# Two of the first four token blocks turned by DMA, the first weights on ScalarE's queue, in a four-layer network of linear attention and gated MLPs

## Chip, cores, metric

The kernel runs on one core of a Trainium2 chip. The metric is the device time of one execution in microseconds (us), where lower is better. The profiler's span is about 1.8 us shorter than that time.

## The reference

The input is one sequence of 2048 tokens of 1024 bf16 values. Four layers follow each other, with a residual addition around each:

```python
x = x + A(layernorm(x), wqkv, wo)              # linear attention, 32 heads of 32
x = x + B(layernorm(x), W_gate, W_up, W_down)  # relu(x Wg) * (x Wu), then W_down; F = 3584
x = x + A(layernorm(x), wqkv, wo)
x = x + B(layernorm(x), W_gate, W_up, W_down)

def A(x, wqkv, wo):
    q, k, v = split_heads(x @ wqkv)
    pq, pk = phi(q), phi(k)                    # phi(t) = (t + 1 if t > 0 else exp(t)) + 1e-6
    kv = einsum("bhsd,bhse->bhde", pk, v); z = pk.sum(s)
    o = einsum("bhqd,bhde->bhqe", pq, kv) / (einsum("bhqd,bhd->bhq", pq, z) + 1e-6)
    return merge_heads(o) @ wo
```

## The kernel before

TensorE does the matmuls, VectorE and ScalarE the elementwise work, and SyncE and ScalarE issue the DMA transfers here. PSUM is the memory that TensorE's results are written to. Tokens are held in 16 blocks of 128, four blocks to a quarter. A block is normalized (two statistics instructions, a combination, two ScalarE steps for the reciprocal root, a scaling) and turned, so that features lie on partitions. Then a "unit" of eight matmuls projects one block onto 512 columns. k00 is block 0 on the first half of the key columns, k10 is block 1 on the same, q00 is block 0 on the first half of the query columns. The weight tiles are k0, k1, q0, q1 and v0, 1 MB each. x0 to x15 are the blocks' inputs, 256 KB each.

The change touches the head only. That is the first quarter of the first layer, some 40 us of 1629:

```python
# head(): idle matmuls, then the first loads
for _ in range(10):
    nc.tensor.matmul(idle, lhsT=zero[:, 0:P], rhs=zero, start=True, stop=True)
k0, k1, v0, q0, q1 = (ring.place() for _ in range(5))
self.load_x(0, 0, nc.scalar)          # half of x0, ScalarE's queue
self.load_x(0, 1)                     # other half, SyncE's queue
self.load_x(1, None, nc.scalar)
k0(0, H)                              # SyncE
self.load_x(2, None, nc.scalar)
k0(H, 2 * H)
self.load_x(3, None, nc.scalar)
k1(); q0()
self.load_x(4); ... ; self.load_x(7)
q1()
for t in range(8, self.ST): self.load_x(t)
v0()
...
# head_units(): the order of the work on blocks 0 to 3
def block0():
    stat(0, 0); stat(0, 1); rstd(0)
    stat(1, 0)                        # x1's first statistics AHEAD of x0's scaling
    scale(0, 0); scale(0, 1)
    t0 = turn(0, 0); t1 = turn(0, 1)  # transposes on TensorE, then copied out of PSUM
    ...
    k(0, 0, between)
def block(j, c, n):                   # used for n = 2 and 3
    scale(n)
    t0 = turn(n, 0); t1 = turn(n, 1)
    t0("s"); t1("s")
    if n + 1 < QT: norm(n + 1)
    k(j, c)
return [block0, block1, lambda: k(0, 1), lambda: block(1, 1, 2), lambda: k(2, 0),
        lambda: block(2, 1, 3), lambda: k(3, 0), lambda: k(3, 1)]
...
# quarter0(): the head units, then all eight query units of the first quarter
run(first)
run(column_major(q_unit, 0))
```

Blocks 4 to 15 are turned by DMA in both kernels (a DMA transpose issued by SyncE).

Of the kernel before, what the change touches and what calls it, by code (L numbers as in the profile page):

```python
# [15 lines left out]
QT = 4  # L16


class _Ring:
# [9 lines left out]
    def place(self):  # L29

        name, src = self.plan[self.loaded]
        t = self.pool.tile([P, 8, NW], BF16, tag="w")
        self.tiles[name] = t
        self.loaded += 1
        return lambda lo=0, hi=8: self.nc.sync.dma_start(out=t[:, lo:hi, :], in_=src[:, lo:hi, :])

    def load_to(self, n):
        while self.loaded < min(n, len(self.plan)):
# [40 lines left out]
class _Net:  # L79
# [131 lines left out]
    def head(self):  # L211

        nc, tc, ring = self.nc, self.tc, self.ring
        H = self.KT // 2

        zero = self.ep.tile([P, NW], BF16, tag="e")
        nc.vector.memset(zero, 0.0)
        idle = self.ps3.tile([P, NW], F32, tag="b")
        for _ in range(10):
            nc.tensor.matmul(idle, lhsT=zero[:, 0:P], rhs=zero, start=True, stop=True)  # L220

        k0, k1, v0, q0, q1 = (ring.place() for _ in range(5))
        self.load_x(0, 0, nc.scalar)
        self.load_x(0, 1)
        self.load_x(1, None, nc.scalar)
        k0(0, H)
        self.load_x(2, None, nc.scalar)
        k0(H, 2 * H)
        self.load_x(3, None, nc.scalar)
        k1()  # L230
        q0()
        self.load_x(4)
        self.load_x(5)
        self.load_x(6)
        self.load_x(7)
        q1()
        for t in range(8, self.ST):
            self.load_x(t)
        v0()
        src = self.xb  # L240
        self.xnT[0, 0] = self.xnTp.tile([P, self.KT, QT * P], BF16, tag="xnT", name="xnT0_0")
        stats = [self.small.tile([P, 2, nc.vector.BN_STATS_DIM], F32, tag="stats", name=f"st{j}")
                 for j in range(QT)]
        rs, xn = {}, {}

        def stat(j, c):
            self.ln_stat(j, src[j], c, stats[j])

        def rstd(j):
            rs[j] = self.ln_rstd(stats[j])  # L250
            xn[j] = self.xn_home(0, j)

        def scale(j, h=None):
            self.ln_scale(src[j], *rs[j], xn[j], h)

        def turn(j, h):
            tp = self.ps3.tile([P, H, P], BF16, tag="b")
            for i in range(H):
                kt = h * H + i
                nc.tensor.transpose(tp[:, i, :], xn[j][:, kt * P:(kt + 1) * P], self.ident)  # L260
            dst = self.xnT[0, 0][:, h * H:(h + 1) * H, j * P:(j + 1) * P]

            def take(engine):
                if engine == "v":
                    nc.vector.tensor_copy(out=dst, in_=tp)
                else:
                    nc.scalar.activation(out=dst, in_=tp, func=ACT.Copy)

            return take

        return stat, rstd, scale, turn

    def head_units(self, k, stat, rstd, scale, turn):

        def block0():
            stat(0, 0)
            stat(0, 1)
            rstd(0)
            stat(1, 0)
            scale(0, 0)  # L280
            scale(0, 1)
            t0 = turn(0, 0)
            t1 = turn(0, 1)
            t0("s")
            stat(1, 1)
            rstd(1)
            t1("v")
            k(0, 0, between)

        def between():  # L290

            scale(1, 0)
            t0 = turn(1, 0)
            scale(1, 1)
            t0("v")

        def block1():
            turn(1, 1)("v")
            norm(2)
            k(1, 0)  # L300

        def norm(j):
            stat(j, 0)
            stat(j, 1)
            rstd(j)

        def block(j, c, n):
            scale(n)
            t0 = turn(n, 0)
            t1 = turn(n, 1)  # L310
            t0("s")
            t1("s")
            if n + 1 < QT:
                norm(n + 1)
            k(j, c)

        return [block0, block1, lambda: k(0, 1), lambda: block(1, 1, 2), lambda: k(2, 0),
                lambda: block(2, 1, 3), lambda: k(3, 0), lambda: k(3, 1)]

    def ln_turn(self, layer, t, xn):  # L320
        nc = self.nc
# [60 lines left out]
    def layer_A(self, l, last_ln):  # L382
        nc, G, KT, D = self.nc, self.G, self.KT, self.D
        ring, later = self.ring, self.later
        H = D // NW
# [23 lines left out]
        def k_unit(q, j, c, between=None):  # L409
            t = q * QT + j  # L410
            pk = self.pk_home(l, t)
            self.phi(project(f"k{c}", q, j, between), pk[:, c * NW:(c + 1) * NW], "v")
            later.at(1 + (10 if self.phi_lag else 0), lambda: k_sum(t, slice(c * NW, (c + 1) * NW)))
# [54 lines left out]
        def q_unit(sc, j, c, lag=None):  # L468
            if c == 0 and (sc, j) not in pq_of:
                if sc < self.NQ - 1:  # L470
                    a = self.xnTp.tile([P, QT, D], BF16, tag="xnT", name=f"pq{l}_{sc}")
                    for i in range(QT):
                        pq_of[sc, i] = a[:, i, :]
                else:
                    pq_of[sc, j] = self.xnp.tile([P, D], BF16, tag="xn", name=f"pq{l}_{sc}_{j}")
            pq = pq_of[sc, j]
            self.phi(project(f"q{c}", sc, j), pq[:, c * NW:(c + 1) * NW], "s" if sc < self.NQ - 1 else "v")
            if c == H - 1 and lag is not None:
                later.at(lag, lambda: z_mult(sc, j))
# [61 lines left out]
        def column_major(f, q):  # L541
            return [lambda j=j, c=c: f(q, j, c) for c in range(H) for j in range(QT)]
# [4 lines left out]
        def run(*lists):  # L547

            n = max(len(u) for u in lists)
            for i in range(n):  # L550
                for u in lists:
                    if i < len(u):
                        u[i]()
                        later.tick()

        if l == 0:
            steps = self.head()
# [2 lines left out]
        for i in range(QT, self.ST):  # L560
            self.ln_at((8 if l == 0 else 2) + 3 * (i - QT), l, i, 2)
        if l == 0:
            first = self.head_units(lambda *a: k_unit(0, *a), *steps)
        else:
            first = column_major(k_unit, 0)

        def quarter0():
            self.phi_lag = 3 if l == 0 else 0
            run(first)
            run(column_major(q_unit, 0))  # L570
            later.at(1, lambda: None)
            self.phi_lag = 0

        if l == 0:
            with self.tc.manual_schedule(engines={mybir.EngineType.DVE,
                                                  mybir.EngineType.Activation}):
                quarter0()
        else:
            run(first, column_major(q_unit, 0))
# [160 lines left out]
```

## Time and profile before

| | kernel before |
|---|---|
| median of the runs ahead of the prediction | 1629.3 us (1629.21 to 1630.51) |
| the profiled run | 1630.68 us, span 1628.9 us |
| TensorE busy | 1621.7 us |
| TensorE idle, whole run | 7.2 us, of which 4.0 us in the first 10.3 us and 2.95 us after the last matmul |

The prediction shows the lines of the profile. To read them: a row of the timeline has the start, the duration, the engine, the source line, the operation and its tiles, the count, and in square brackets how long the engine had been idle and what ended that. A row of waits has who waited for whom, the total, the number of times and the longest, in us.

### The profile page before, as it was taken

What the parts mean: (1) busy time and instruction counts of PE and PEld (TensorE: products, weight loads), DVE (VectorE), ACT (ScalarE), POOL (GpSimd) and SP (SyncE); (2) the same over time, 40 slices, a digit from 0 to 9 for tenths busy, and PEclk for the clock granted to TensorE, in tenths of its full rate; (3) what the DMA queues carried; (4) which work ended last, traced back from release to release, by engine and by line L of the source; (5) the groups of instructions that cost most, each with busy time, mean ns of one, the idle gap of its engine ahead of it and who ended that gap; (6) DMA issues with size and microseconds to landing.
All of it is one profiled execution on the core that took longest, in us unless ns stands there. A gap on an engine that the chain in (4) does not pass through costs nothing.

```text
span 1628.9 us, 18772 instructions
## 1 busy us (share of the span) xinstructions
PE 1621.7 (100%) x7754; PEld 739.3 (45%) x7754; DVE 566.7 (35%) x940; ACT 331.8 (20%) x638; POOL 201.9 (12%) x134
## 2 busy tenths in 40 slices
PE   8999999999999999999999999999999999999999
PEld 4444444444444444444444444444444444444444
DVE  7845695213212222212165547942022111111211
ACT  5741212101110110111066312121011101101110
POOL 2349220000000000000023592100000000000000
DMA  7312647448445444544560147464554454454452
GB/s 245 65 52 56 178 71 206 144 148 232 155 143 190 160 151 161 168 147 137 168 128 1 53 93 250 85 193 146 182 165 152 155 184 155 145 166 154 155 162 71
DMA packets 298246, 235.06 MB, mean 144 GB/s; under 512 B 101296, under 2 KB 294192, under 8 KB 298160
## 3 DMA queue, kind: packets, MB, share of 16 engines
q1 hardware_dynamic: 292832, 228.75, 47.7%
q10 hardware_dynamic: 5328, 5.11, 0.9%
q8 instruction: 60, 0.98, 0.3%
q14 instruction: 26, 0.21, 0.0%
HBM read 201.33 MB, written 8.39 MB: 129 GB/s over the span
## 4 chain that ended last, share of the span: by engine, by line
PE 98%; ACT 1%; DVE 1%; DMA 1%; issue 0%; SPq 0%; DVEq 0%
PE pu L639 24%; PE pg L639 24%; PE acc L663 23%; PE ps L404 12%; PE ps L530 7%; PE ps L439 7%; DMA t<-in_A_wqkv_dram 1%; PE kv L452 0%; PE acc_last L663 0%; ACT e L351 0%; ACT e L350 0%; PE fold L515 0%; DVE st L138 0%; ACT e L352 0%; DVE slab L358 0%
## 5 line engine op out<-in xcount | busy, mean ns | idle before, releaser
L639 PEld LDWEIGHTS <-t 128*128 128x128 bf16 x3584 | 350.3, 98 | 423.2
L639 PE MATMUL pu<-xnT,t 128*128 128x512 bf16 x1792 | 423.5, 379 | 0.0
L639 PE MATMUL pg<-xnT,t 128*128 128x512 bf16 x1792 | 423.4, 379 | 0.0
L663 PE MATMUL acc<-t,hT 128*128 128x512 bf16 x1764 | 382.5, 379 | 0.0
L645 DVE TENSOR_TENSOR hT<-pu,rg 128x512 bf16<-128x512 f32 x224 | 154.7, 691 | 572.0 <-PE pu L639 572.0
L644 ACT ACTIVATE rg<-pg 128x512 f32<-128x512 f32 x224 | 133.5, 596 | 737.3 <-PE pg L639 737.0
L663 PEld LDWEIGHTS <-hT 128*128 128x128 bf16 x1820 | 177.9, 98 | 209.1
L404 PE MATMUL ps<-t,xnT 128*128 128x512 bf16 x1024 | 224.3, 380 | 2.2 <-DMA t<-in_A_wqkv_dram 1.7
L404 PEld LDWEIGHTS <-xnT 128*128 128x128 bf16 x1024 | 99.2, 98 | 122.3 <-issue 4.3
L530 PE MATMUL ps<-T,pqT 128*128 128x512 bf16 x512 | 111.2, 379 | 0.0
L145 ACT ACTIVATE rstd<-mv,eps 128x1 f32<-128x1 f32 x64 | 18.7, 293 | 334.1 <-DVE mv L143 333.9
L680 DVE TENSOR_TENSOR xo<-x,acc 128x512 bf16<-128x512 f32 x31 | 21.3, 688 | 170.3 <-PE acc L663 170.3
L483 POOL TENSOR_TENSOR prod<-pq,zrow 128x1024 f32<-128x1024 bf16 x32 | 67.9, 2122 | 85.9 <-DVE den L488 72.5
L138 DVE BATCH_NORM_STATS2 stats<-x 128x6 f32<-128x512 f32 (+1 forms) x120 | 78.0, 673 | 0.8
L530 PEld LDWEIGHTS <-pqT 128*128 128x128 bf16 x512 | 49.9, 98 | 60.4 <-issue 0.5
L419 POOL CAST ksum<-x 128x512 f32<-128x512 bf16 x2 | 1.7, 866 | 605.4 <-DVE x L358 605.4
L677 DVE TENSOR_TENSOR x<-x,acc 128x512 f32<-128x512 f32 x32 | 21.6, 675 | 138.5 <-PE acc L663 137.4
L421 POOL TENSOR_TENSOR ksum<-ksum,slab 128x512 f32<-128x512 f32 x46 | 54.0, 1183 | 84.6 <-DVE slab L358 75.1
L358 DVE SCALAR_TENSOR_TENSOR pq<-ps,e 128x512 bf16<-128x512 f32 x64 | 44.0, 688 | 53.9 <-ACT e L352 52.2
L495 POOL TENSOR_TENSOR pq<-pq,den 128x1024 bf16<-128x1024 bf16 x32 | 61.7, 1933 | 3.1 <-DVE den L490 3.1
L488 DVE TENSOR_REDUCE den<-prod 128x32 f32<-128x1024 f32 x32 | 39.0, 1217 | 53.9 <-POOL prod L483 53.9
L439 PE MATMUL ps<-slab,x 128*128 128x512 bf16 x256 | 56.6, 379 | 0.0
(57 smaller groups left out, 596.0 us busy)
## 6 DMA issues: line engine op xcount, KB each, us to landing
t<-in_B_W_gate_dram SPq DMA_DIRECT2D x56, 1024.0 KB, 7.1
t<-in_B_W_up_dram SPq DMA_DIRECT2D x56, 1024.0 KB, 5.4
t<-in_B_W_down_dram SPq DMA_DIRECT2D x64, 896.0 KB, 5.2
t<-in_A_wqkv_dram SPq DMA_DIRECT2D x11, 1024.0 KB, 5.6
t<-in_A_wo_dram SPq DMA_DIRECT2D x4, 1024.0 KB, 7.2
away<-x SPq DMA_DIRECT2D x8, 512.0 KB, 4.4
x<-away SPq DMA_DIRECT2D x8, 512.0 KB, 8.5
out_dram<-xo ACTq DMA_DIRECT2D x31, 128.0 KB, 2.5
```

Of the source, the lines that this page charges most:

```text
L138: self.nc.vector.bn_stats(out=stats[:, c, :], in_=src[:, c * fmax:(c + 1) * fmax])
L358: nc.vector.scalar_tensor_tensor(out=out, in0=ps, scalar=0.0, in1=e, op0=ALU.max, op1=ALU.add)
L404: nc.tensor.matmul(by_row(ps), lhsT=self.xnT[l, l_q][:, kt, j * P:(j + 1) * P], rhs=w[:, kt, :].rearrange("p (b i d) -> p i b d", i=R, d=H ...
L421: nc.gpsimd.tensor_tensor(out=ksum[:, cols], in0=ksum[:, cols], in1=pk, op=ALU.add)
L439: nc.tensor.matmul(ps, lhsT=self.xn[l, t][:, d * P:(d + 1) * P], rhs=self.pk[l, t][:, h * NW:(h + 1) * NW], start=(t == 0), stop=(t == sel ...
L483: nc.gpsimd.tensor_tensor(out=prod, in0=pq_of[sc, j], in1=zrow, op=ALU.mult)
L495: nc.gpsimd.tensor_tensor(out=heads(pq), in0=heads(pq), in1=den[:, :].unsqueeze(2).to_broadcast([P, D // HD, HD]), op=ALU.mult)
L530: nc.tensor.matmul(ps, lhsT=pqT[sc][:, g, j * P:(j + 1) * P], rhs=T[g // 2][:, g % 2, n2 * NW:(n2 + 1) * NW], start=(g == 0), stop=(g == G ...
L639: nc.tensor.matmul(ps, lhsT=w[:, kt, fi * P:(fi + 1) * P], rhs=self.xnT[l, q][:, kt, :], start=(kt == 0), stop=(kt == KT - 1))
L644: nc.scalar.activation(out=rg, in_=pg, func=ACT.Relu)
L645: nc.vector.tensor_tensor(out=h[:, fi, :], in0=pu, in1=rg, op=ALU.mult)
L663: nc.tensor.matmul(ps[:, 0:n], lhsT=hT[ft // 4][:, ft % 4, j * P:(j + 1) * P], rhs=wd[:, k, i * n:(i + 1) * n], start=(ft == 0), stop=(ft ...
```

## The change

The intent is to give the first weights the DMA engines early, to take 16 transposes off TensorE, and to have other work (two query units) ready while blocks 2 and 3 are turned by DMA. Cut to the core:

```diff
         k0, k1, v0, q0, q1 = (ring.place() for _ in range(5))
-        self.load_x(0, 0, nc.scalar)
+        self.load_x(0, 0)
         self.load_x(0, 1)
-        self.load_x(1, None, nc.scalar)
-        k0(0, H)
-        ... (x2, x3 on ScalarE's queue; k0, k1, q0, x4 to x15, q1, v0 on SyncE's)
+        self.load_x(1)
+        nc.vector.memset(ring.get((0, "k0"))[:, 0, 0:2], 0.0)
+        k0(0, H, nc.scalar)
+        k0(H, 2 * H, nc.scalar)
+        k1(0, 2 * H, nc.scalar)
+        q0(0, 2 * H, nc.scalar)
+        def load(n):
+            if n == 0:
+                nc.vector.memset(self.xb[2][:, 0:2], 0.0)   # holds x2 back
+                self.load_x(2)
+                self.load_x(3)
+                return
+            for t in range(4, 8):
+                self.load_x(t)
+            q1()
+            for t in range(8, self.ST):
+                self.load_x(t)
+            v0()
...
         def block0():
             stat(0, 0)
+            load(0)
             stat(0, 1)
...
-        def block(j, c, n):            # ... transposes on TensorE
+        def turned(n):
             scale(n)
+            self.ln_turn(0, n, xn[n])  # DMA transpose
-        return [block0, block1, lambda: k(0, 1), lambda: block(1, 1, 2), ...]
+        return ([block0, block1, lambda: (turned(2), norm(3), k(0, 1)),
+                 lambda: (turned(3), load(1), k(1, 1)), lambda: q(0, 0), lambda: q(1, 0)]
+                + [lambda f=f, j=j, c=c: f(j, c) for j in (2, 3) for f, c in ((k, 0), (k, 1), (q, 0))]
+                + [lambda j=j: q(j, 1) for j in range(QT)])
```

SyncE's order in this stretch is now the program's own, as VectorE's and ScalarE's were already.

More of the change, by code (lines that the diff above doesn't have):

```diff
@@ L34, in place @@
         self.loaded += 1
-        return lambda lo=0, hi=8: self.nc.sync.dma_start(out=t[:, lo:hi, :], in_=src[:, lo:hi, :])
+        return lambda lo=0, hi=8, queue=None: (queue or self.nc.sync).dma_start(
+            out=t[:, lo:hi, :], in_=src[:, lo:hi, :])
     def load_to(self, n):
@@ L222, in head @@
         k0, k1, v0, q0, q1 = (ring.place() for _ in range(5))
-        self.load_x(0, 0, nc.scalar)
+        self.load_x(0, 0)
         self.load_x(0, 1)
-        self.load_x(1, None, nc.scalar)
-        k0(0, H)
-        self.load_x(2, None, nc.scalar)
-        k0(H, 2 * H)
-        self.load_x(3, None, nc.scalar)
-        k1()
-        q0()
-        self.load_x(4)
-        self.load_x(5)
-        self.load_x(6)
-        self.load_x(7)
-        q1()
-        for t in range(8, self.ST):
-            self.load_x(t)
-        v0()
+        self.load_x(1)
[16 more added lines that the diff above has]
+            v0()
         src = self.xb
@@ L269, in turn, with head_units @@
             return take
-        return stat, rstd, scale, turn
-    def head_units(self, k, stat, rstd, scale, turn):
+        return load, xn, stat, rstd, scale, turn
+    def head_units(self, k, q, load, xn, stat, rstd, scale, turn):
         def block0():
             stat(0, 0)
+            load(0)
             stat(0, 1)
@@ L305, in norm @@
             rstd(j)
-        def block(j, c, n):
+        def turned(n):
             scale(n)
-            t0 = turn(n, 0)
-            t1 = turn(n, 1)
-            t0("s")
-            t1("s")
-            if n + 1 < QT:
-                norm(n + 1)
-            k(j, c)
-        return [block0, block1, lambda: k(0, 1), lambda: block(1, 1, 2), lambda: k(2, 0),
-                lambda: block(2, 1, 3), lambda: k(3, 0), lambda: k(3, 1)]
+            self.ln_turn(0, n, xn[n])
[3 more added lines that the diff above has]
+                + [lambda j=j: q(j, 1) for j in range(QT)])
     def ln_turn(self, layer, t, xn):
@@ L562, in layer_A @@
         if l == 0:
-            first = self.head_units(lambda *a: k_unit(0, *a), *steps)
+            first = self.head_units(lambda *a: k_unit(0, *a), lambda *a: q_unit(0, *a), *steps)
         else:
@@ L569, in quarter0 @@
             run(first)
-            run(column_major(q_unit, 0))
-            later.at(1, lambda: None)
             self.phi_lag = 0
         if l == 0:
-            with self.tc.manual_schedule(engines={mybir.EngineType.DVE,
+            with self.tc.manual_schedule(engines={mybir.EngineType.DVE, mybir.EngineType.SP,
                                                   mybir.EngineType.Activation}):
```

## The prediction

> **What bounds the kernel now.** I read the page first (busy shares and chain), then the wait totals, then the timeline of the first 22 us, because the change touches nothing later, and last the landings of the single loads in that stretch.
>
> ```profile
> PE 1621.7 (100%) x7754; PEld 739.3 (45%) x7754; DVE 566.7 (35%) x940; ACT 331.8 (20%) x638; POOL 201.9 (12%) x134
> ...
> PE 98%; ACT 1%; DVE 1%; DMA 1%; issue 0%; SPq 0%; DVEq 0%
> ```
>
> TensorE is busy for 1621.7 of 1628.9 us. All the idle time there is to win is 7.2 us, 0.44%. The whole-run waits say where TensorE spends it:
>
> ```profile
> PE ps L404 <- DMA t<-in_A_wqkv_dram: 1.7, 1, 1.7
> PE idle L220 <- DVE zero L217: 1.3, 1, 1.3
> ...
> PE tp L260 <- DVE x L154: 0.6, 1, 0.6
> ...
> PE ps L404 <- ACT xnT L267: 0.4, 1, 0.4
> ```
>
> These sum to 4.0 us. The chain of waits ends its matmuls at 1625.95, so 2.95 us more are the tail, the last addition and store, which the change does not touch. Of 7.2 us only the 1.7 us wait for the first weights and the 0.6 and 0.4 us ahead of the first block are within the change's reach. The timeline shows that stretch:
>
> ```profile
> 6.38 0.72 PE L260 MATMUL tp<-ident,x 128*128 128x128 bf16 x8 [0.58 <-DVE x L154]
> ...
> 7.46 1.04 PE L404 MATMUL ps<-t,xnT 128*128 128x512 bf16 x4 [0.37 <-ACT xnT L267]
> ...
> 10.23 0.59 PE L404 MATMUL ps<-t,xnT 128*128 128x512 bf16 x2 [1.73 <-DMA t<-in_A_wqkv_dram]
> ...
> 11.56 3.74 PE L404 MATMUL ps<-t,xnT 128*128 128x512 bf16 x16
> ...
> 15.13 0.61 PE L260 MATMUL tp<-ident,x 128*128 128x128 bf16 x8
> ...
> 15.58 3.62 PE L404 MATMUL ps<-t,xnT 128*128 128x512 bf16 x16
> ...
> 19.28 0.62 PE L260 MATMUL tp<-ident,x 128*128 128x128 bf16 x8
> ```
>
> Four matmuls of the first unit use the first half of weight tile k0, then 1.73 us are lost until the second half lands. The two groups of 8 transposes at 15.13 and 19.28 are those of blocks 2 and 3. The next projection starts at 15.58 and at 19.74, so each group holds TensorE for 0.45 us. A projection unit of 8 matmuls takes 1.73 us (0.216 us each).
>
> The landings of the two halves of k0 (queries on the load line, cut to one or two loads each) are:
>
> ```profile
> L35 SPq DMA_DIRECT2D t<-in_A_wqkv_dram x1: 419/419/419, 1.2 to 1.2; - x1
> DMA to landing us min/median/max: 4.5/4.5/4.5
> ...
> L35 SPq DMA_DIRECT2D t<-in_A_wqkv_dram x2: 419/460/500, 1.2 to 1.7; - x2
> DMA to landing us min/median/max: 4.5/6.5/8.5
> ```
>
> So k0's halves landed at 5.7 and 1.66 + 8.5 = 10.2 us. The same query gives, for the others: k1 2.2 + 11.2 = 13.4, q0 3.6 + 12.8 = 16.4; blocks of tokens x1 5.2, x2 1.7 + 7.7 = 9.4, x3 2.2 + 8.2 = 10.4, x4 5.75 + 11.3 = 17.05. The windows of 1 us show the DMA at 302 to 388 GB/s from 3 us on: it is saturated, and which bytes go first decides who waits. Note the third unit, the first to use k1: it follows the second unit at about 13.4, just as k1 lands. So k1 is nearly a bound already.
>
> **What the Trainium skill says.** "DMA: Bandwidth & Descriptors", section "Issuing engines are not separate DMA queues": transfers started by ScalarE and SyncE run on the same 16 engines and interleave; a second issuer saves issue time only. The trace agrees: two queues were in use and the sum stayed below 390 GB/s. The same page, "Queues, rings and completion order": an engine alternates between queues packet by packet, and completion is not first-in-first-out. The trace agrees: k0's second half was complete only when 2.8 MB had moved (sum of the windows to 10.2 us), although just 2.1 MB (four blocks and k0) had been asked for ahead of it or with it. The same page, "Rules for kernel authors": a transpose next to ordinary DMAs needs nothing, only two transposing queues must be kept apart. Here all are issued from SyncE; the first transpose of the trace landed after 4.1 us with loads in flight, a later one after 3.0. "TensorE: Matmul & The Clock Gate", Part 4, puts a transpose at about 275 ns in one kernel; here 8 hold TensorE for 0.45 us together, so 56 ns each, and the measurement decides.
>
> **The change part by part.**
> 1. Blocks 2 and 3 are turned by DMA. TensorE loses 16 transposes: 2 x 0.45 = 0.90 us, all on its path. ScalarE loses 4 copies (two pairs of 1.08 us), off the path.
> 2. The order becomes k00, k10, k01, k11, q00, q10 (six units on blocks 0 and 1), then k, k, q of block 2, of block 3, then the four second-half query units. The same 16 units; in the instruction order of the changed kernel TensorE differs only by the 16 transposes. ScalarE's three-step query work (0.60 + 0.63 + 0.72 = 1.95 us a unit, above 1.73) is now mixed with one-step key units; before, it ran 8 in a row and the only gap later in the head, 0.11 us at 44, may be its effect. Gain 0.1.
> 3. Weights k0, k1, q0 go on ScalarE's queue; x0 and x1 go on SyncE's, x2 and x3 are held back by a tiny memset until the first statistics (about 4.3 us: x0's half lands at 3.54, plus 0.65 of statistics and the memset). The first half of k0 waits for a memset too, so it starts at about 1.4 instead of 1.19.
>
> Landings by my estimate: fit to the before landings, the slowest engine moves as if the whole ran at 0.30 MB/us from 2.1 us, plus 0.6 us to land (k0b: 2.1 MB gives 9.7, seen 10.2; k1: 3.15 MB gives 13.2, seen 13.4; q0: 4.2 MB gives 16.7, seen 16.4). After, k0b needs 1.57 MB (x0, x1, k0) plus 0 to 0.5 of x2 and x3: 7.9 to 9.7. k1 needs 2.6 to 3.15 MB: 11.4 to 13.2. q0 needs 4.2 MB and has no x4 beside it: about 16.4.
>
> Now TensorE's clock. k00 starts at about 7.5 (x1 is issued 0.35 us later and its statistics stand ahead of x0's scaling, so 0 to 0.3 later, partly balanced by earlier statistics of x0). Without a wait for k0b, k00 and k10 with block 1's transposes (2 x 0.22) end at 7.46 + 3.46 + 0.44 = 11.4. k01 needs k1: at 12.8, a new wait of about 1.4. k01 and k11 end at 16.3; q00 needs q0 at 16.4. q00 and q10 end at 19.9. Block 2's first unit starts there. Before, six units with the same transposes plus those of two blocks were done at 19.74 + 1.73 = 21.47. Gain 1.5 us, plus the 0.1: 1.6. Had the weights been there in time it would have been 1.73 + 0.90 + 0.1 = 2.7.
>
> Is block 2 turned by 19.9? x2 issued at 4.3 lands perhaps at 10 (the 4.0 to 7.7 us of x1 and x2 before). Then statistics 1.28, combining 0.21, the two ScalarE steps 0.5, scaling 0.55: scaled at 12.6; DMA transpose 4.1 to 4.7 us under load: 17.3. Slack 2.6 us. Block 3 is scaled near 16, turned near 20, needed at 25. But VectorE's order puts the statistics of blocks 2 and 3 ahead of freeing the first unit's PSUM: x2's landing + 5.2, so 15.2, needed by q00 at 16.4. If x2 lands at 12, this costs 0.7. The loads of x4 on are held until block 3's transpose is issued (about 17 instead of 5.75): x4 lands near 20.5, its statistics come at about 21.7; q1 lands near 26, needed at 30.3. Both fit, with 1 and 4 us of slack.
>
> I take off 0.1 for such small losses: gain 1.5 us. 1629.3 - 1.5 = 1627.8.
>
> **The rivals.**
> - The wait only moves: k0b's 1.7 us is given back in full at k1 and q0, because the same 4.2 MB are needed and now the query weights are asked for about 5 us sooner (after four units, not eight). For it: q0's 16.4. It leaves the transposes' share or less: gain 0.5 to 1, about 1628.6.
> - VectorE or the DMA transposes become the bound: x2 held back by 2.6 us lands at 12 to 13 (7.7 after issue), PSUM comes free late or block 2 is late. Against it: x2 stands first in an empty SyncE queue. Gain 0 to 0.5, or a loss up to 1: 1629 to 1630.
> - The transfers go better than the estimate: 4.2 MB at the mean 365 GB/s would have q0 by 14.2, k1 by about 11.5. Gain 2.7, 1626.6.
> - The late start of x4 to x15 stalls the second quarter. Against it: 12 blocks, q1 and v0 (5.2 MB) take about 15 us from 19, so land by 35, and the second quarter starts at 37.
>
> **Range and chances.** The bound of 2.7 us gives 1626.6 at best, a full loss gives 1629.3, and a bad head 1630; the three runs before spread by 1.3 us. Range 1626.3 to 1629.6. Two per cent is 32.6 us: the change can't win that, as only 7.2 us are idle, and I see nothing in it to lose as much, so within 2% at 0.985.
>
> **What would show it.** Right: TensorE busy falls by 0.9 us; the 1.7 us wait for weights shrinks to under 0.6 in the first unit and one of about 1 us appears at the third; the sixth unit ends near 20. Wrong: a TensorE wait on the transposed tile at the seventh unit (block 2 late), on VectorE's join at the fifth (PSUM), a first unit starting after 8, or the third unit starting at 11.5 without a wait (then the gain is near 2.7).

## The result

| | before | changed |
|---|---|---|
| median of 4 runs | 1629.32 us (1629.21 to 1630.51) | 1632.71 us (1630.74 to 1634.47) |
| granted clock, run by run | | 0.999, 0.998, 1.000, 0.999 |
| ratio changed / before | | 1.0019, interval 1.0001 to 1.0036 |

The change did not gain 1.5 us. It lost about 3, and the predicted range, which ended at 1629.6, does not hold the median. The spread grew with it, to 3.7 us.

The busy share of TensorE in the changed kernel, from the page:

```profile
PE 1621.6 (99%) x7738; PEld 739.7 (45%) x7738; DVE 566.9 (35%) x942; ACT 331.1 (20%) x634; POOL 201.9 (12%) x134
```

There are 16 matmuls fewer, but busy time fell by only 0.1 us, where the prediction had 0.9 less. Other matmuls must have run more slowly. The waits of TensorE in the first 60 us of the changed kernel:

```profile
PE tp L267 <- DVE x L155: 2.1, 1, 2.1
...
PE ps L408 <- DMA xnT<-x: 1.9, 1, 1.9
...
PE idle L221 <- DVE t L228: 1.3, 1, 1.3
...
PE ps L408 <- ACT xnT L274: 0.4, 1, 0.4
...
PE ps L408 <- DVE slab L362: 0.3, 1, 0.3
```

The 1.7 us wait for weights is gone, and no wait for weights took its place. Instead the wait ahead of the first transposes grew from 0.6 to 2.1 us. A wait of 1.9 us for a tile turned by DMA is new, and so is 0.3 us for VectorE (PSUM not yet freed). TensorE's timeline of the changed kernel puts them in place:

```profile
1.35 4.04 PE L221 MATMUL idle<-zero 128*128 128x512 bf16 x10 [1.35 <-DVE t L228]
7.51 0.72 PE L267 MATMUL tp<-ident,x 128*128 128x128 bf16 x8 [2.13 <-DVE x L155]
8.60 2.74 PE L408 MATMUL ps<-t,xnT 128*128 128x512 bf16 x6 [0.37 <-ACT xnT L274]
...
12.28 5.35 PE L408 MATMUL ps<-t,xnT 128*128 128x512 bf16 x24
17.98 21.15 PE L408 MATMUL ps<-t,xnT 128*128 128x512 bf16 x96 [0.35 <-DVE slab L362]
41.03 69.24 PE L408 MATMUL ps<-t,xnT 128*128 128x512 bf16 x320 [1.90 <-DMA xnT<-x]
110.11 8.80 PE L443 MATMUL ps<-slab,x 128*128 128x512 bf16 x40
```

The same stretch in the kernel before, from its sixth unit on:

```profile
19.74 88.70 PE L404 MATMUL ps<-t,xnT 128*128 128x512 bf16 x408
108.27 8.80 PE L439 MATMUL ps<-slab,x 128*128 128x512 bf16 x40
```

The last row of each is the stage after the keys and queries. Before, it started at 108.27, now at 110.11, which is 1.84 us later. The spans differ by 1.9 us (1628.9, 1630.8). So all of the difference arises ahead of this stage, and its start can serve as the measure in the experiments.

Three things are to be seen. First, the start: the first transposes begin at 7.51 instead of 6.38. VectorE's timeline says why:

```profile
4.41 0.21 DVE L144 BATCH_NORM_AGGREGATE mv<-st 128x2 f32<-128x12 f32 x1
...
6.45 0.69 DVE L139 BATCH_NORM_STATS2 st<-x 128x6 f32<-128x512 bf16 x1 [1.83 <-DMA x<-in_A_x_dram]
7.06 0.72 DVE L155 TENSOR_SCALAR x<-x,mv,rstd 128x512 bf16<-128x512 bf16 x2
```

x0 was ready to be scaled at about 5.2. VectorE waited until 6.45 for x1, whose statistics stand ahead in its order. x1 was third on SyncE's queue, issued at 1.66 and landed 4.8 us later. Before, it was second on ScalarE's queue and landed at 5.2.

Second, six projection matmuls take 2.74 us, where the same six before took 1.04 + 0.59 besides the wait. The 1 us windows of the changed kernel show the granted TensorE clock as the column behind the five engines:

```profile
8.00:9.00 1.00, 0.63 (x5) 0.19 (x4) 0.88 (x3) 0.85 (x3) 0.00 (x0) 0.63 1.07 371
9.00:10.00 1.00, 1.00 (x4) 0.44 (x3) 0.73 (x2) 0.19 (x1) 0.00 (x0) 0.50 1.04 363
10.00:11.00 1.00, 1.00 (x4) 0.30 (x3) 0.00 (x0) 0.00 (x0) 0.00 (x0) 0.50 1.09 358
11.00:12.00 1.00, 1.00 (x7) 0.67 (x6) 0.20 (x1) 0.00 (x0) 0.00 (x0) 0.67 1.09 347
```

Together (0.37 + 0.50 + 0.50 + 0.33) / 0.5 = 3.4 us at half clock. Third, the 17th unit, the first of block 4, waits for its turned block. The first DMA transpose of block 4 in the kernel before, then in the changed one, by duration of the issue (ns), time of issue, and time to landing:

```profile
L326 SPq DMA_TRANSPOSE xnT<-x x1: 1347/1347/1347, 27.2 to 27.2; - x1
DMA to landing us min/median/max: 4.1/4.1/4.1
```

```profile
L330 SPq DMA_TRANSPOSE xnT<-x x1: 4813/4813/4813, 31.7 to 31.7; - x1
DMA to landing us min/median/max: 9.3/9.3/9.3
```

It was issued 4.5 us later and took 5.2 us longer, behind x8 to x15 and v0 in the same queue (v0 was issued at 30.95 and landed at 39.4). The late issue was not VectorE's doing, since block 4 was scaled by 27.9. SyncE works in order, and its own waits (20 to 46 us) show what held it:

```profile
SPq L373 <- DMA t<-in_A_wqkv_dram: 3.2, 1, 3.2
...
SPq L35 <- DMA x<-in_A_x_dram: 0.3, 1, 0.3
SPq L330 <- DMA x<-in_A_x_dram: 0.3, 1, 0.3
```

The program takes the semaphores of SyncE's DMAs from eight in turn, so each waits for the landing of the one eight places ahead of it. x15 waited for q1 (landed at 30.25), v0 for x8 (30.93), and the transpose for x9 (31.61). In the kernel before, the last of these waits ended at 23.5, before block 4 was ready (27.2).

From start to start, the two traces differ as follows, with 1.727 us a unit (8 x 0.2158):

| term | worked out | us |
|---|---|---|
| first transposes later | 7.51 - 6.38 | +1.13 |
| from there to k10, without the wait for weights | (12.28 - 7.51) - (11.56 - 6.38 - 1.73): half clock | +1.32 |
| no wait for k0's second half | | -1.73 |
| no 16 transposes | 2 x 0.45 | -0.90 |
| small waits around them, before | (19.74 - 11.56) - 4 x 1.727 - 0.90 | -0.37 |
| PSUM, changed | (17.98 - 12.28) - 3 x 1.727 | +0.52 |
| 17th unit late | 41.03 - (17.98 + 12 x 1.727) | +2.33 |
| later gaps, before less changed | 69.08 - (108.27 - 19.74 - 11 x 1.727) | -0.45 |
| sum | | +1.85 |

The measured sum is +1.84. The 17th unit's 2.33 is from start to start; the trace, which models the ends of matmuls, shows 1.90 of it as idle.

### The profile page after: what moved, and what is told of

It reads as the page before. It is cut to its first block, busy times and chain, and to the rows that moved or that the text cites. A ratio compares the mean times of both kernels' runs of the same rounds, so it can differ in the third digit from the quotient of the medians.

```text
span 1630.8 us, 18741 instructions
## 1 busy us (share of the span) xinstructions
PE 1621.6 (99%) x7738; PEld 739.7 (45%) x7738; DVE 566.9 (35%) x942; ACT 331.1 (20%) x634; POOL 201.9 (12%) x134
## 4 chain that ended last, share of the span: by engine, by line
PE 98%; DMA 1%; DVE 1%; ACT 0%; issue 0%; SPq 0%; DVEq 0%
PE pu L641 24%; PE pg L641 24%; PE acc L665 23%; PE ps L408 12%; PE ps L534 7%; PE ps L443 7%; DMA xnT<-x 1%; PE kv L456 0%; PE acc_last L665 0%; DMA x<-in_A_x_dram 0%; PE fold L519 0%; DVE x L155 0%; DVE st L139 0%; DVE slab L362 0%; DVE e L360 0%
```

## The experiments

The changed kernel was not timed in the call of e1 to e4, so their medians are set against it across calls, between which its own median moved from 1632.71 to 1634.22; their profiles are the firmer evidence. "Clock" counts the runs whose recorded mean granted clock was 1.000.

| run | edit, in words | median (low to high) | clock 1.000 | before on the same chip |
|---|---|---|---|---|
| e1_x1_early | changed, x1 ahead of the weights | 1630.32 (1629.36 to 1632.03) | 3 of 5 | 1630.00 (1629.42 to 1630.64) |
| e2_warm | changed, 19 idle matmuls | 1630.50 (1630.29 to 1631.40) | 5 of 5 | same |
| e3_loads_late | changed, last loads later | 1631.19 (1630.70 to 1632.68) | 1 of 5 | same |
| e4_both | e1 and e3 | 1630.51 (1629.09 to 1631.25) | 3 of 5 | same |
| after_again | changed, unaltered | 1634.22 (1632.30 to 1635.67) | 2 of 5 | 1629.37 (1629.27 to 1630.93) |
| e5_scale_first | changed, x0 scaled before x1's statistics | 1632.25 (1629.76 to 1632.81) | 2 of 5 | same |
| e6_before_hold | before, x2 and x3 held | 1630.56 (1628.88 to 1630.84) | 2 of 5 | same |
| e8_best | changed, repaired | 1629.16 (1629.06 to 1629.20) | 5 of 5 | same |
| before_a, before_b | before, unaltered, one look each | 1629.44; 1630.60 | 1.000; 0.999 | 1629.51 (1629.20 to 1630.70) |
| e9_best_nofill | e8 without its extra idle matmuls | 1629.19 (1628.65 to 1629.99) | 4 of 5 | same |
| e10_hold_warm | before, x2 and x3 held, 13 idle matmuls | 1629.32 (1628.93 to 1629.37) | 5 of 5 | same |
| after_c, d, e, f | changed, unaltered, one look each | 1631.36; 1630.43; 1629.17; 1632.22 | 0.999; 0.999; 1.000; 1.000 | 1630.08 (one run) |

### e1_x1_early: x1 ahead of the weights

```diff
         self.load_x(0, 0)
-        self.load_x(0, 1)
-        self.load_x(1)
+        self.load_x(0, 1, nc.scalar)
+        self.load_x(1, None, nc.scalar)
```

> The changed kernel with one edit: the second half of x0 and x1 are issued on ScalarE's queue ahead of the weights, as before the change. Theory (x1 late): in the changed kernel x1 landed at 6.45 instead of 5.2, VectorE's statistics of x1 stand ahead of the scaling of x0, so TensorE sat idle 2.13 us and then ran some 3.4 us at half clock. Then here x1 lands by 5.3, the first transposes start at 6.3 to 6.7 (7.51 in the changed kernel), the clock of the head is full, and the time falls by 1.1 to 2.5 us to about 1630.0; the wait of about 1.9 us for block 4's DMA transpose at the 17th unit stays, because VectorE's chain moves with the start. Rival (late start is bandwidth of the weights, whatever the queue): x1 still lands after 6 and the start stays above 7.3, time unchanged near 1632.5. Rival (the loss is all at the 17th unit): the start moves but the 17th unit starts at 41 as before, time unchanged.

In the profile x1 landed at 4.1, the first transposes began at 6.64, the clock was full, the stage after the keys began at 106.88 and the span was 1627.5 us. In that execution k01 waited 1.13 us for k1, as the prediction had it. The 1.9 us at the 17th unit did not stay, contrary to what was expected: block 4's transpose landed at 37.7. The other runs were less kind. Two of five, at clock 0.999, took 1631.7 and 1632.0. So the late x1 is a cause, but putting x1 first is no cure by itself. The timeline of this run shows a new cost:

```profile
1.68 3.89 ACTq L35 DMA_DIRECT2D t<-in_A_wqkv_dram  x4
...
4.63 0.21 DVE L144 BATCH_NORM_AGGREGATE mv<-st 128x2 f32<-128x12 f32 x1
...
5.61 0.29 ACT L146 ACTIVATE rstd<-mv,eps 128x1 f32<-128x1 f32 x1 [3.60 <-DVE st L139]
```

The statistics were ready at 4.84, but ScalarE was issuing q0, its last of six loads, until 1.68 + 3.89 = 5.57. An engine that issues loads does nothing else while it does.

### e2_warm: more idle matmuls

```diff
-        for _ in range(10):
+        for _ in range(19):
```

> The changed kernel with 19 idle matmuls at the start instead of 10, so that TensorE is busy until about 7.3 and the gap ahead of the first transposes shrinks from 2.1 us to under 0.5; nothing is issued or landed earlier. Theory (the idle gap makes the granted clock fall): the clock of the windows from 8 to 12 us is 1.00 instead of 0.5 to 0.67, the six first projection matmuls take 1.3 instead of 2.74 us, the granted clock of every run is 1.000, the time is 1630.7 to 1631.2 and the spread of the runs falls from 3.7 us to under 1. Rival (half clock comes by chance of the executions, not from this gap): clock and spread stay as they were, 1630.7 to 1634.5.

TensorE's timeline:

```profile
1.34 6.04 PE L221 MATMUL idle<-zero 128*128 128x512 bf16 x19 [1.34 <-DVE t L228]
7.64 0.72 PE L267 MATMUL tp<-ident,x 128*128 128x128 bf16 x8 [0.26 <-DVE x L155]
8.73 1.47 PE L408 MATMUL ps<-t,xnT 128*128 128x512 bf16 x6 [0.36 <-ACT xnT L274]
```

The start was no earlier than in the changed kernel's profile (7.64), but the six matmuls took 1.47 us instead of 2.74, all five runs were at clock 1.000, and the spread was 1.1 us (under 1 was expected, and a median of 1630.7 or more). With the gap filled and nothing else changed, the half clock is gone, so the idle gap causes it. The wait at the 17th unit stayed (2.1 us).

### e3_loads_late: block 4's transpose ahead of the last loads

```diff
-            for t in range(4, 8): ...; q1(); for t in range(8, self.ST): ...; v0()
+            if n == 1:      # x4 to x7, q1, x8 to x11
+                ...
+                return
+            for t in range(12, self.ST):
+                self.load_x(t)
+            v0()
...
-                + [lambda j=j: q(j, 1) for j in range(QT)])
+                + [lambda j=j: q(j, 1) for j in range(QT - 1)]
+                + [lambda: (q(QT - 1, 1), load(2))])
```

> The changed kernel with the loads of x12 to x15 and of v0 issued after the 16th unit, behind the first DMA transposes of the second quarter. Theory (block 4's transpose was issued at 31.67 behind loads in SyncE's queue and landed after 9.3 us at 41.0): here it is issued near 28, lands within 5 us, TensorE's wait of 1.9 us at the 17th unit is gone (under 0.3), and the time falls by about 1.9 us from the changed kernel's 1632.7, to 1629 to 1631 with the half clock at the start still there. Rival (a DMA transpose under these conditions is slow by itself, or VectorE is late with block 4): the wait stays over 1 us, time unchanged.

Block 4's transpose was issued at 27.3 and landed at 36.0, so it was still slow (8.7 us where under 5 was expected), but in time. What the edit took away was the hold on SyncE, not the slow landing. There is no gap at the 17th unit:

```profile
18.29 36.69 PE L413 MATMUL ps<-t,xnT 128*128 128x512 bf16 x168 [0.37 <-DVE slab L367]
```

The stage after the keys began at 108.75, where the changed kernel's began at 110.11, although this start was no better (7.62, half clock). The wait was a matter of what stands ahead in the queue. The time, 1631.19, is just above the range expected.

### e4_both

> Both edits: x0's second half and x1 on ScalarE's queue ahead of the weights, and x12 to x15 and v0 issued after the 16th unit. If the late x1 and the late transpose explain the loss, the two savings add and the change's own gains (no wait for k0's second half 1.73, no 16 transposes 0.90) come out, less some 0.35 to 1 for PSUM and weights: 1627.2 to 1628.4, 1 to 2 us below the kernel before (1629.3), granted clock 1.000. If something else in the new order costs the time, it stays at 1629.3 or above.

It missed: 1630.51, no better than the kernel before. In its profile the 17th unit has no wait, but ScalarE was held by q0's issue until 5.96, the first transposes began at 7.04 and the half clock came again (2.23 us for the six matmuls). The two causes were real, but the first repair brought a third cost with it.

### after_again: the changed kernel on the second call's chip

> The changed kernel itself, unaltered, so that it is timed on the same chip and against the same runs of the kernel before as the other kernels of this call. If the half clock after the 2.1 us gap depends on where a clock window of some 3.4 us lies, the runs fall apart: those at granted clock 1.000 at 1630.5 to 1631, those at 0.999 and 0.998 1.7 and 3.5 us longer; median 1631 to 1633, kernel before 1629.3 to 1630.0. If the losses were a matter of the first chip, it is within 0.5 us of the kernel before.

The median was 1634.22 against 1629.37, ratio 1.0026 (1.0014 to 1.0039), so the loss is not a matter of one chip. That is above the 1631 to 1633 expected. In the profile x1 landed at 7.1 and the gap ahead of the transposes was 2.76 us. The half clock came twice, from 8 to 12 us and again from 42 to 46 us, the second time behind the 2.03 us wait at the 17th unit. Two runs over 1634 had a recorded clock of 1.000, which this account did not explain. after_f bears on that below.

### e5_scale_first: VectorE's order alone

```diff
             rstd(0)
-            stat(1, 0)
             scale(0, 0)
             scale(0, 1)
+            stat(1, 0)
```

> The changed kernel with one swap in VectorE's order: x0 is scaled before the first statistics of x1, no load is touched. Theory (x1 is late, and costs time only because its statistics stand ahead of x0's scaling): x1 still lands at 6.4 or later, but the first transposes start at 5.6 to 6.3 instead of 7.5, the gap ahead of them is under 0.8 us instead of 2.1, the granted clock is 1.000 in nearly all runs; x1's own transposes come at about 9, k01 then waits up to 1 us for k1 (lands at 12.3). The wait for block 4's transpose at the 17th unit stays at about 1.5. Time 1629.3 to 1630.3. Rival (the start is set by something else, ScalarE's weight issues or the first half of k0): the first transposes stay after 7, or the first projection stays after 8.3.

This was half right, and the time, 1632.25, missed the 1629.3 to 1630.3 expected. x1 landed at 6.7, and the first transposes no longer waited for it, but they began at 6.88 rather than by 6.3. The second half of x0, now second on SyncE's queue, landed at 4.9 in this execution, and VectorE waited 1.35 us for it. The half clock still came in three of five runs. The order in VectorE carries the delay of x1, but it is not the only late load.

### e6_before_hold: holding x2 and x3 in the kernel before

```diff
-        self.load_x(2, None, nc.scalar)   # and x3
...
             stat(0, 0)
+            self.held()                   # tiny memset on x2, then x2 and x3 on ScalarE's queue
```

> The kernel before with one idea of the change alone: x2 and x3 are held by the tiny memset until the first statistics of x0 are done, everything else, transposes on TensorE and queues too, as before. Theory (the 1.7 us wait for k0's second half comes from x2 and x3 sharing the DMA engines, but the weights as a whole are bound by k1): k0's second half lands at 8.5 to 9 instead of 10.2, its wait falls below 0.7, and 0.9 to 1.5 us of wait for k1 (landing 12.3 to 13.4) or for block 2 turn up at the third unit instead; time within 0.6 us of the kernel before. Rival (priority of k0 is worth its full 1.7 us): 1.5 us faster than the kernel before.

In its profile k0's second half landed at 7.3, k1 at 11.6, and TensorE waited for weights 0.2 us in all, so k1 did not become the bound as I had expected. Even so the two runs at full clock took 1628.88 and 1629.28 against 1629.37. If the priority were worth 1.7 us, they would be at 1627.7. That contradicts the profile that the prediction rested on, and led to the next two runs.

### before_a and before_b: the kernel before, looked at twice more

> The kernel before, unaltered, profiled once more. The trace that the prediction was made from was of a run of 1630.68 us, 1.4 us over the median of 1629.3. Theory: the 1.73 us wait for k0's second half is a matter of that run; a run near 1629.3 shows a wait of under 0.7 us, k0's second half landing before 9.2 instead of 10.2, and the stage after the keys starting near 106.9 instead of 108.3. Rival: the wait is 1.5 us or more in a run of 1629.3 too, and the 1.4 us lie elsewhere (half clock, or the tail).

> The same a second time, since one profile is one execution: as in the run ahead of it. If one of the two is near 1630.5 and the other near 1629.3, the first-weights wait and the granted clock of the first 45 us tell the two apart.

TensorE's timeline of the run of 1629.44 us:

```profile
6.53 0.72 PE L260 MATMUL tp<-ident,x 128*128 128x128 bf16 x8 [0.74 <-DVE x L154]
7.62 1.04 PE L404 MATMUL ps<-t,xnT 128*128 128x512 bf16 x4 [0.36 <-ACT xnT L267]
8.96 0.59 PE L404 MATMUL ps<-t,xnT 128*128 128x512 bf16 x2 [0.30 <-DMA t<-in_A_wqkv_dram]
```

And of the run of 1630.60 us:

```profile
1.34 3.77 PE L220 MATMUL idle<-zero 128*128 128x512 bf16 x10 [1.34 <-DVE zero L217]
6.49 0.72 PE L260 MATMUL tp<-ident,x 128*128 128x128 bf16 x8 [1.38 <-DVE x L154]
7.58 2.65 PE L404 MATMUL ps<-t,xnT 128*128 128x512 bf16 x6 [0.37 <-ACT xnT L267]
```

In both, k0's second half landed at 9.0 (10.2 in the first profile). The wait for it, "1.73 us" in the prediction's trace, is 0.30 us in a run near the median and nothing in the other. The stages after the keys began at 107.22 and 108.38. In the second run the idle matmuls ended 0.7 us early, since the last of them already ran at full rate; the gap was longer, and the kernel before, too, fell to half clock. So the kernel before has good runs near 1629.3 and worse ones near 1630.5, and the trace that I predicted from was of the worse kind.

### e8_best: the repaired kernel

```diff
-        self.load_x(0, 1)
+        self.load_x(0, 1, nc.scalar)
         self.load_x(1)
...
             rstd(0)
+            load(-1)                    # q0 on ScalarE's queue only now
...
-        for _ in range(10):
+        for _ in range(12):
...                                      # 6 idle matmuls ahead of k01; x12 to x15, v0 as in e3
```

> The changed kernel with its losses taken out: x0's second half first on ScalarE's queue and x1 second on SyncE's, so that x1 lands by 4.5 to 5.3; q0 issued on ScalarE only after the first two steps of x0's normalization, so that its issue (which held ScalarE until 5.5 to 6.0 in the run with x1 early) does not delay them; x12 to x15 and v0 after the 16th unit; 12 idle matmuls at the start and 6 ahead of the third unit to keep the clock up while k1 is awaited. If these are the causes: first transposes at 5.6 to 6.5, granted clock 1.000 in all runs, third unit at k1's landing (12.3 to 13.3), 17th unit at 36.5 to 37.7 without a wait, time 0.8 to 1.8 us under the kernel before on the same chip, spread under 1 us. If a cause is missing, it stays within 0.5 us of the kernel before.

```profile
6.21 0.72 PE L281 MATMUL tp<-ident,x 128*128 128x128 bf16 x8
7.29 1.50 PE L424 MATMUL ps<-t,xnT 128*128 128x512 bf16 x6 [0.37 <-ACT xnT L288]
...
11.27 1.46 PE L236 MATMUL idle<-zero 128*128 128x512 bf16 x6
12.57 40.32 PE L424 MATMUL ps<-t,xnT 128*128 128x512 bf16 x184
```

The mechanism is as expected: the start is at 6.21, x1 landed at 4.4, k01 began as k1 landed (12.5), and there is no wait at the 17th unit. All five runs are at full clock, within 0.14 us of each other, and each lies under each of the nine runs of the kernel before (1629.06 to 1629.20 against 1629.27 to 1630.93). The gain is small, though: 0.2 us of the median and 0.7 us of the mean (1629.14 against 1629.85), ratio 0.9995 with the interval 0.9983 to 1.0008, which the test does not tell from no change. I had expected 0.8 to 1.8 us.

### e9_best_nofill and e10_hold_warm

e9 is e8 with 10 idle matmuls at the start and none ahead of k01. e10 is e6 with 13 instead of 10.

> The repaired kernel without its idle matmuls: 10 at the start as in the changed kernel and none ahead of the third unit. Theory (idle gaps of about 0.5 us at 5.8 and of 1.3 us at 11 let the clock fall in some runs): some of the five runs are at granted clock 0.999 and 1.3 to 1.8 us longer, median 1629.2 to 1630.8, spread over 1.2 us, against 0.14 us with them. Rival (the clock falls only after the gap of 2 us of the changed kernel): five runs within 0.4 us of 1629.1.

> The kernel before with x2 and x3 held (as in the earlier experiment) and 13 idle matmuls at the start instead of 10; transposes on TensorE as before. The earlier run without more idle matmuls had two runs at full clock (1628.88, 1629.28) and three at 0.999 (1630.6 to 1630.8). Theory (the only bad luck is the clock at the start): all runs at 1.000 and 1628.7 to 1629.3, at least 0.2 us under the kernel before and no worse than the repaired kernel with DMA transposes (1629.16), which would mean that turning by DMA is worth nothing. Rival: the clock still falls in some runs, from the later gaps.

e9 lies between the two theories: one run of five at clock 0.999 and 1629.99, the others from 1628.65 to 1629.20, median 1629.19. The fillers seem to remove the bad run and to cost something in the best ones, but five runs each, on two chips, do not settle that. e10 came nearly as expected: all at full clock, 1628.93 to 1629.37, 0.19 us under the kernel before in the median. With transposes still on TensorE it is within 0.2 us of the repaired kernel (other chip, kernel before at 1629.51 there against 1629.37). That does not mean that turning by DMA saves nothing on TensorE. In the profiles, the stretch from k01 to the stage after the keys took 94.97 us in e10 (12.20 to 107.17) and 94.14 in e8 (12.57 to 106.71), so 0.83 less, near the 0.90 foretold. But k01 began 0.37 us later in e8, as k1 landed later (12.5 against 12.2). So 0.46 us remained at the start of that stage in these two executions, and 0.16 us in the medians.

### after_c to after_f: what made the long runs long

> The changed kernel, profiled again: so far its two profiled runs (1632.57 at clock 0.999, 1634.84 at 0.998) both showed the half clock, but two of five timed runs took 1634.1 to 1634.2 at a recorded clock of 1.000, which the half clock does not explain. Theory (late landing of x1, and the wait for block 4's transpose that follows from it): a run at clock 1.000 and over 1633 shows the first projection after 9.5 or the 17th unit after 42. Rival (the record's mean clock hides it): such a run shows windows at half clock all the same.

> As the run ahead of it: another execution of the changed kernel. Whatever its time, the start of the stage after the keys less 108.3 gives its distance from the kernel before's first profile, within 0.4 us.

> As the two ahead of it: another execution. If all losses are the four named (late start, half clock, PSUM, block 4's transpose), they sum to the difference of the stage start within 0.5 us here too.

> As the three ahead of it: another execution; if one run of the four is near 1630.7 at clock 1.000, it shows a gap ahead of the first transposes under 2 us and no window at half clock, with the wait of about 2 us at the 17th unit still there.

The best of them, after_e at 1629.17 us, shows TensorE's timeline as the change must have intended it:

```profile
6.89 0.72 PE L267 MATMUL tp<-ident,x 128*128 128x128 bf16 x8 [1.10 <-DVE x L155]
7.98 1.47 PE L408 MATMUL ps<-t,xnT 128*128 128x512 bf16 x6 [0.36 <-ACT xnT L274]
...
12.29 24.74 PE L408 MATMUL ps<-t,xnT 128*128 128x512 bf16 x112 [0.20 <-DMA t<-in_A_wqkv_dram]
37.27 15.71 PE L408 MATMUL ps<-t,xnT 128*128 128x512 bf16 x72 [0.24 <-DMA xnT<-x]
```

Here x1's statistics began at 5.83 instead of 6.45, the clock held, and the 17th unit waited 0.24 us. In after_c and after_d there was no wait at the 17th unit, but the half clock was there. In after_f (1632.22 us, recorded clock 1.000) the timeline and the clock column disagree; first TensorE's timeline, then the window of 9 to 10 us:

```profile
7.75 1.03 PE L267 MATMUL tp<-ident,x 128*128 128x128 bf16 x8 [1.96 <-DVE x L155]
9.05 2.74 PE L408 MATMUL ps<-t,xnT 128*128 128x512 bf16 x6 [0.26 <-ACT xnT L274]
```

```profile
9.00:10.00 1.00, 0.95 (x3) 0.40 (x4) 0.79 (x3) 0.40 (x2) 0.00 (x0) 1.00 1.06 369
```

The six matmuls took 2.74 us, exactly as at half clock, with a granted clock of 1.00 in the view. The trace shows why: its first clock record of this execution is at 13.86 us, and ahead of the first record the view shows 1.00. (In every run it does so for the first idle matmuls too, which start 0.427 us apart, where 0.216 is full rate.) In after_f the idle matmuls, the transposes (0.107 us apart, 0.056 at full rate) and the projections all keep half rate until then. So here the clock did not fall in the gap: it had not risen yet. The rival was right in that the recorded mean can miss the half clock, and the count of runs at clock 1.000 is an upper bound of the good runs. None of the four runs was over 1633 at clock 1.000, as the expectation had asked. The two runs over 1634 no longer contradict the account, but they were not profiled, so that they are of this kind is inferred.

The stage after the keys began at 109.12, 108.19, 106.94 and 110.00 in these four; less 108.3 that is 0.8, -0.1, -1.4 and 1.7. The spans less the 1628.9 of the first profile are 0.7, -0.3, -1.5 and 1.5: agreed within 0.2, as expected of after_d. For after_e the table's method gives +0.51 for the late start, nothing for half clock, +0.80 for PSUM and the 17th unit together, and +0.37 for a fifth loss that the expectation had not listed, the wait for k1.

The half clock can therefore be read from the spacing of the matmuls. The table has, for all eighteen profiles, the time from the end of the idle matmuls to the first projection (only transposes lie in it), and whether any of the first six projections ran at half rate (1.47 to 1.63 us for the six is full rate, 2.08 and more is not; in after_c and after_d the first three were still at full rate):

| time without a projection or idle matmul, us | rate of the first six |
|---|---|
| 0.91 (e10), 1.02 (e8), 1.35 (e2), 1.58 (e9), 1.66 (e6), 1.67 (before), 1.83 (before_a), 1.94 (e1), 2.18 (after_e) | full in all nine |
| 2.40 (after_d), 2.47 (before_b), 2.54 (e4), 2.68 (e5), 2.94 (after_c), 3.08 (e3), 3.21 (after), 3.26 (after_f), 3.92 (after_again) | half, in part or all, in all nine |

The two sides do not overlap. TensorE's idle time ahead of the transposes alone separates them as well (1.10 us and less, 1.31 us and more). But the length of a gap is not the whole rule: at the 17th unit 2.0 us brought half clock in after_again, while 1.9 to 2.1 us did not in the changed kernel's first profile, e2 and e5, nor did a wait of 1.73 us between projections in the first profile of the kernel before.

The clock records in the traces, which the windows only average, explain this. All nine half-clock stretches recorded in the heads are 3.41 us long, and within a trace the changes lie whole multiples of 3.41 us apart. Cut into such stretches, the first 60 us of the traces divide by how long TensorE was on matmuls other than transposes, counted from their spacing: a clock that was up fell at the end of each stretch with 0.3 to 1.2 us of them, and stayed up after each with 1.3 us or more (once, in the tail of e5, also after 1.2 us). At the 17th unit it was 1.21 us in after_again (39.11 to 42.53) and 1.35 us in the changed kernel's first profile (38.97 to 42.38). So what a gap does depends on where it lies in the stretches, and that differed between executions. Transposes do not seem to count: with them, after_d would have 1.42 us in the stretch after which its clock fell, more than the 1.35 us after which it stayed up. (The first profile of the kernel before has no clock record, and after_f none before 13.86.)

## Why the prediction was wrong

By its own steps:

- **What could be won.** "Of 7.2 us only the 1.7 us wait for the first weights and the 0.6 and 0.4 us ahead of the first block are within the change's reach" was read from one execution at 1630.68 us, and the gain was then taken off the median of 1629.3. In a run near the median the wait for k0's second half is 0.30 us. The term "Gain 1.5 us" was thus mis-sized by 1.3 to 1.4 us before anything else: in before_a the sixth unit starts at 18.46, not 19.74. The best execution of the changed kernel (1629.17) is 0.27 us ahead of before_a (1629.44).
- **The start.** "k00 starts at about 7.5 (...) so 0 to 0.3 later" failed. In the result's trace it started at 8.60, past the 8 that the prediction itself had named as a sign of being wrong. I saw the order of VectorE, but took x1's landing to move with its issue, by 0.35 us (the issue moved by 0.47). It moved from 5.2 to 6.4 there, and lay between 5.8 and 7.1 in the six executions of the changed kernel that were profiled. e5 shows that the order passes the delay on, and e1 that the start matters.
- **The clock.** The prediction did not have it. It noted 0.6 us of idle time ahead of the first block and did not ask what a longer gap does. e2 shows it: same late start, no gap, no half clock. It cost 1.32 us in the result's trace.
- **The second quarter.** "Both fit, with 1 and 4 us of slack" was about the loads of x4 and q1 and held only just: they landed at 23.1 and 30.3, not 20.5 and 26, and x4's statistics waited 0.2 us. The rival "the late start of x4 to x15 stalls the second quarter" was put aside because the loads would land by 35 and the quarter starts at 37. v0 landed at 39.4. And I had not followed the next step: the DMA transposes stand in the same queue behind those loads. Block 4's was held at SyncE until 31.67, 3.8 us after the block was ready, and landed after the loads, at 41.0. It cost 1.9 to 2.3 us in the result's trace; e3 removes it. In other executions it cost 0 to 2.0 us.
- **What held.** The wait for k0 fell away. The landings were near the estimate: k1 12.3 (estimate 12.8), x2 10.0 (10), q0 15.2 (16.4). Block 2's turning (18.7 against 17.3) and VectorE's PSUM hand-over were seen as the tight places, and PSUM cost 0.3 to 0.5 us. The wait for k1 at the third unit (about 1.4) showed in e1 as 1.13 and in after_e as 0.20; in the result's trace the late start hid it.
- **Within 2%.** That was right, and for the reason given.

So the expected gain went three ways. Most of it had not been there in a typical run. What was there was given back by the late start with its half clock, and by the wait at the 17th unit. How much the DMA turning is worth by itself was not measured with the start and the queues exactly alike; e8 against e10 has 0.83 us less from k01 on, and 0.2 us in the medians.

## What to carry to other kernels

Predict from a trace whose own time is near the median, or profile twice: a wait of 1.7 us in one execution may be 0.3 in the next. When loads are reordered, ask for each one who stands behind it in every in-order queue, the DMA queue and VectorE's program alike; here x1 held x0's scaling, and the loads ahead of it held a transpose, at its issue and in its landing. At the start of a kernel, keep TensorE on matmuls until real work is there, and judge the clock by the spacing of the matmuls, not by the record alone.

## What the Trainium skill lacked or had wrong

- "TensorE: Matmul & The Clock Gate", section "Why this matters for your kernels", asks for no idle gaps over about 3 us. 2.40 us without a matmul other than transposes was followed by half clock, as was every longer such time at the start, and 2.18 us was not. So 3 us is too generous here. What separated the cases was the work inside a stretch of 3.41 us: the clock fell after 1.2 us of matmuls or less and stayed after 1.3 us or more.
- The same page, section "Seeing it yourself", warns that clock events in a trace are unreliable. The first profile of the kernel before bears it out: it has no clock record at all, although its matmuls go from 0.427 to 0.216 us apart. A trap of the view comes on top: ahead of the first record, in after_f at 13.86 us, it shows 1.00 while six matmuls take 2.74 us, against 1.47 at full clock.
- The same page, Part 4, gives about 275 ns for a transpose. That is how long one lasts (0.22 us here); it does not say what a row of them costs, and eight in a row hold TensorE for 0.45 us here, 56 ns each.
- "DMA: Bandwidth & Descriptors", section "Rules for kernel authors", says that a transpose next to ordinary DMAs needs nothing. I take that to be about correctness; of time that row says nothing, and behind loads in its own queue a transpose landed after 9.3 us instead of 4.1.
- The same page, section "Issuing engines are not separate DMA queues", calls the issue time usually small relative to the DMA itself. So it was (in e1 3.89 us of issuing for four loads that took 5.5 to 13.0 us to land), but not small for the engine: ScalarE was held from 1.68 to 5.57 us and was late for its own next step by 0.8 us.
